# LayerScale on one core: the stores released by VectorE's third-piece product and not by a load's landing

## Chip, cores and metric

One core of a Trainium2 chip runs the kernel. The metric is the device time of one execution in microseconds (us); lower is better. Before the change the median of three runs is 119.76 us (119.63 to 119.88). No host time is in it.

## The reference

```python
B, S, D = 1024, 16, 512          # all bfloat16
def reference(x, y, gamma):      # x, y: (B, S, D), gamma: (D)
    return x + gamma * y
```

x, y and the output are 16.78 MB each. The kernel must read 33.56 MB and write 16.78 MB of HBM, and it does one product and one sum per element.

## The kernel before

The tensors are seen as 16384 rows of 512 elements, 128 for each partition. "Rows 4 to 68" below are rows of this count in a partition. `BLOCKS` cuts the 128 into blocks of 4, 64 and 60 rows; inside a block each partition's rows are contiguous in HBM, so a transfer of rows 4 to 68 is 128 runs of 64 KB. `PIECES` cuts the same 128 rows for VectorE: pieces 0 to 4 are rows 0 to 8, 8 to 24, 24 to 68, 68 to 120 and 120 to 128.

Nothing is scheduled: every engine's order is written out by hand.

- `SP` lists the transfers that SyncE issues, in order: y 0 to 4, y 4 to 68, x 4 to 68, y 68 to 128, x 68 to 120, x 120 to 128. `ACT` lists those of ScalarE's queue: x 0 to 4, gamma, and then the three stores, rows 4 to 68, 0 to 4 and 68 to 128. ScalarE computes nothing. The profile calls SP's DMA queue q1 and ScalarE's q10.
- `y_sb` holds all 128 rows of y, is multiplied and added to in place, and is what the stores read. `x_sb` has no room for all of x: the last number of an x load is its place there. x 68 to 120 goes where rows 24 to 68 (piece 2) lay, and x 120 to 128 where piece 0's lay; `frees` makes these loads wait for the sums of those pieces (`s_add`).
- `DVE` lists VectorE's instructions: products ("m") of pieces 0, 1, 2, sums ("a") of 2, 0, 1, products of 3 and 4, sums of 3 and 4. A product is line 180, a sum line 189. Each waits for its load by a semaphore (`need`), and a sum waits for the products before it (`s_dve`).
- TensorE broadcasts gamma to all partitions by a matmul with ones (L152), and VectorE copies the result to `gamma_sb` (L154).
- `ring` issues one engine's transfers. A store waits for `s_go` once, ahead of the first store, and for as many sums in `s_add` as its rows need. For the first store these are three sums, for the last all five.

`RELEASE` names what sets `s_go`. Before, it is the load of x's rows 68 to 120. TensorE waits for that load and passes it on, to ScalarE (`s_go`) and to VectorE (`s_rel`), whose sum of piece 3 needs the same load:

```python
    _take(s_load[RELEASE], 16, nc.tensor)
    nc.tensor.sem_inc(s_go, 1)
    nc.tensor.sem_inc(s_rel, 1)
```

`_take` waits for a semaphore and takes the count off again. At the end SyncE waits for ScalarE's end, all sums and all three stores.

Of the kernel before, what the change touches and what calls it, by code (L numbers as in the profile page):

```python
# [22 lines left out]

HOLD, AHEAD = ('y', 0, 4), (2, 1)

RELEASE = ('x', 68, 120, 24)

DVE = [('m', 0), ('m', 1), ('m', 2), ('a', 2), ('a', 0), ('a', 1), ('m', 3), ('m', 4), ('a', 3), ('a', 4)]
MULT, ADD = mybir.AluOpType.mult, mybir.AluOpType.add


def _take(sem, n, eng):


    return eng.wait_ge(sem, n).then_inc(sem, -n)  # L35


def kernel(
    tc: tile.TileContext,
    x: bass.AP,  # L40
    y: bass.AP,
    gamma: bass.AP,
    out: bass.AP,
):

    nc = tc.nc
    P = nc.NUM_PARTITIONS
    tc.close()  # L50
    tc.compile()  # L51

    xf = x.flatten_outer_dims()
    yf = y.flatten_outer_dims()
    of = out.flatten_outer_dims()
    N, D = xf.shape
    rows = N // P
    n = len(PIECES)
    assert sum(PIECES) == rows
    starts = [sum(PIECES[:c]) for c in range(n + 1)]  # L60
    dt = xf.dtype
    edges = [sum(BLOCKS[:c]) for c in range(len(BLOCKS) + 1)]
    assert edges[-1] == rows

    def rows_of(t, a, b):

        c = max(c for c in range(len(BLOCKS)) if edges[c] <= a)
        assert b <= edges[c + 1]
        block = t[P * edges[c] : P * edges[c + 1]].rearrange("(p n) d -> p n d", p=P)
        return block[:, a - edges[c] : b - edges[c], :]  # L70

    gamma_row = nc.alloc_sbuf_tensor("gamma_row", [1, D], dt).ap()
    ones_row = nc.alloc_sbuf_tensor("ones_row", [1, P], dt).ap()
    gamma_sb = nc.alloc_sbuf_tensor("gamma_sb", [P, D], dt).ap()
    y_sb = nc.alloc_sbuf_tensor("y_sb", [P, rows, D], dt).ap()
    x_loads = [w for w in ACT + SP if w[0] == "x"]
    y_loads = [w for w in SP + ACT if w[0] == "y"]
    stores = [w for w in SP + ACT if w[0] == "s"]
    for loads in (x_loads, y_loads, stores):
        assert sum(w[2] - w[1] for w in loads) == rows  # L80
    x_rows = max(w[3] + w[2] - w[1] for w in x_loads)
    x_sb = nc.alloc_sbuf_tensor("x_sb", [P, x_rows, D], dt).ap()
    gamma_ps = nc.alloc_psum_tensor("gamma_ps", [P, D], mybir.dt.float32).ap()

    sem = nc.alloc_semaphore
    s_gamma, s_ones, s_ps, s_dve = sem("s_gamma"), sem("s_ones"), sem("s_ps"), sem("s_dve")
    s_load = {w: sem("s_" + "_".join(map(str, w[:2]))) for w in x_loads + y_loads}
    s_held = {nc.sync: sem("s_held_sp"), nc.scalar: sem("s_held_act"), nc.vector: sem("s_held_dve")}
    s_add, s_go, s_rel, s_end, s_out = sem("s_add"), sem("s_go"), sem("s_rel"), sem("s_end"), sem("s_out")
    added = [a for kind, *a in DVE if kind == "a"]  # L90
    order = {a[0]: k for k, a in enumerate(added)}

    def meets(a, b, c, d):
        return a < d and c < b

    def pieces_of(a, b):
        return [c for c in range(n) if meets(starts[c], starts[c + 1], a, b)]

    def x_at(row):
        return next(w[3] + row - w[1] for w in x_loads if w[1] <= row < w[2])  # L100

    def frees(w):

        c = set()
        for v in x_loads[: x_loads.index(w)]:
            lo, hi = max(v[3], w[3]), min(v[3] + v[2] - v[1], w[3] + w[2] - w[1])
            if lo < hi:
                c |= set(pieces_of(v[1] + lo - v[3], v[1] + hi - v[3]))
        return sorted(c)

    early = []

    def ring(eng, what, n_early, n_ahead):

        known, went = 0, False
        for k, w in enumerate(what):
            kind = w[0]
            if k == n_ahead:
                _take(s_held[eng], 1, eng)
            need = frees(w) if kind == "x" else pieces_of(w[1], w[2]) + list(w[3:]) if kind == "s" else []  # L120
            need = max((order[c] + 1 for c in need), default=0)
            if kind == "s" and not went:
                _take(s_go, 1, eng)
                went = True
            if need > known:
                eng.wait_ge(s_add, need)
                known = need
            if kind == "g":
                i = eng.dma_start(out=gamma_row, in_=gamma.unsqueeze(0)).then_inc(s_gamma, 16)
            elif kind == "x":  # L130
                to = x_sb[:, w[3] : w[3] + w[2] - w[1], :]
                i = eng.dma_start(out=to, in_=rows_of(xf, w[1], w[2])).then_inc(s_load[w], 16)
            elif kind == "y":
                r = slice(w[1], w[2])
                i = eng.dma_start(out=y_sb[:, r, :], in_=rows_of(yf, w[1], w[2])).then_inc(s_load[w], 16)
            else:
                r = slice(w[1], w[2])
                i = eng.dma_start(out=rows_of(of, w[1], w[2]), in_=y_sb[:, r, :]).then_inc(s_out, 16)
            if k < n_early:
                early.append(i.ins)  # L140

    ring(nc.sync, SP, EARLY[0], AHEAD[0])
    ring(nc.scalar, ACT, EARLY[1], AHEAD[1])


    nc.vector.memset(ones_row, 1.0).then_inc(s_ones, 1)  # L146
    _take(s_load[HOLD], 16, nc.tensor)
    for s_one in s_held.values():
        nc.tensor.sem_inc(s_one, 1)
    _take(s_ones, 1, nc.tensor)  # L150
    _take(s_gamma, 16, nc.tensor)
    nc.tensor.matmul(gamma_ps, ones_row, gamma_row, start=True, stop=True).then_inc(s_ps, 1)  # L152
    _take(s_ps, 1, nc.vector)
    nc.vector.tensor_copy(out=gamma_sb, in_=gamma_ps).then_inc(s_dve, 1)  # L154
    _take(s_dve, 1, nc.vector)

    _take(s_load[RELEASE], 16, nc.tensor)
    nc.tensor.sem_inc(s_go, 1)
    nc.tensor.sem_inc(s_rel, 1)

    landed, open_mults = set(), 0

    def need(loads, c):
        for w in loads:
            if w not in landed and meets(starts[c], starts[c + 1], w[1], w[2]):
                if w == RELEASE:
                    _take(s_rel, 1, nc.vector)
                elif w == HOLD:
                    _take(s_held[nc.vector], 1, nc.vector)
                else:  # L170
                    _take(s_load[w], 16, nc.vector)
                landed.add(w)

    for kind, *args in DVE:
        c = args[0]
        yt = y_sb[:, starts[c] : starts[c + 1], :]
        if kind == "m":
            need(y_loads, c)
            g = gamma_sb[:, None, :].to_broadcast([P, PIECES[c], D])
            nc.vector.tensor_tensor(out=yt, in0=yt, in1=g, op=MULT).then_inc(s_dve, 1)  # L180
            open_mults += 1
        else:
            need(x_loads, c)
            if open_mults:
                _take(s_dve, open_mults, nc.vector)
                open_mults = 0
            at = x_at(starts[c])
            xt = x_sb[:, at : at + PIECES[c], :]
            nc.vector.tensor_tensor(out=yt, in0=xt, in1=yt, op=ADD).then_inc(s_add, 1)  # L189


    nc.scalar.sem_inc(s_end, 1)
    _take(s_end, 1, nc.sync)
    _take(s_add, n, nc.sync)
    _take(s_out, 16 * len(stores), nc.sync)

    main = nc.main_func.blocks[0].instructions
    names = {i.name for i in early}
    for b in nc.main_func.blocks[1:]:
        for i in [i for i in b.instructions if i.name in names]:  # L200
            b.instructions.remove(i)
    for k, i in enumerate(early):
        main.insert(1 + k, i)
# [30 lines left out]
```

## Time and profile before

| what | value |
|---|---|
| median of the runs | 119.76 us |
| the profiled execution: its span, first to last instruction | 118.2 us |
| around the span, by the median | 1.5 us |
| VectorE busy | 70.1 us (59% of the span) |
| DMA queues q1 + q10, share of 16 engines | 64.8% + 33.9% |
| HBM read and written | 33.56 MB, 16.78 MB |
| x 68 to 120: issued, to landing | 55.37, 21.7 us |
| x 120 to 128: issued, to landing | 57.58, 22.0 us |
| stores issued | 77.41, 77.81, 94.43 us |
| sum of piece 3 / of piece 4 start | 78.17 / 92.11 us |

Times of a row are counted from the span's start. The profile shows one execution, whose own time is its span and what lies around it; the median is over other executions. The matmul, the copy and the small memsets together take under 2 us. The DMA share is the busy time of the 16 DMA engines; a transfer of 128 partitions runs on all of them, 8 partitions each. In a window's row the columns are its edges, its length, the busy time and instructions of PE, PEld, DVE and POOL, the granted TensorE clock, the DMA share and GB/s. A DMA packet is counted in the window where it starts, so short windows swing above and below 1.00.

### The profile page before, as it was taken

The numbers are of one execution on the slowest core, as the hardware profiler recorded it, in microseconds if no ns is written. First come the engines' busy times: TensorE is split into PE (matmuls) and PEld (weight loads), VectorE is DVE, ScalarE is ACT, GpSimd is POOL, SyncE is SP. The second block draws the span as 40 slices with busy tenths as digits, with TensorE's granted clock in tenths as the row PEclk, the third lists the DMA queues.
The fourth block names the chain that finished last, engine by engine and source line by source line (L and its number), as shares of the span: only waits on it lengthen the run. The fifth ranks groups of instructions, "written<-read, shape, count | busy, mean of one in ns | idle before, by whom it ended". The sixth has DMA issues, their size and how long they took to land. (4 is left out here: it accounts for less than half of the span.)

```text
span 118.2 us, 91 instructions
## 1 busy us (share of the span) xinstructions
PE 0.6 (0%) x1; PEld 0.1 (0%) x1; DVE 70.1 (59%) x12; POOL 0.2 (0%) x4
## 2 busy tenths in 40 slices
PE   0000100000000000000000000000000000000000
PEld 0000000000000000000000000000000000000000
DVE  0000200089999969999999999999999900000000
POOL 0000000000000000000000000000000000000000
DMA  6999889988899879879969696898899889799793
GB/s 248 461 666 399 355 355 399 665 355 355 355 599 466 355 333 624 374 333 499 499 288 576 288 576 288 360 637 355 355 576 488 355 355 510 333 582 416 333 499 166
DMA packets 1442, 50.33 MB, mean 426 GB/s; under 512 B 161, under 2 KB 162, under 8 KB 546
## 3 DMA queue, kind: packets, MB, share of 16 engines
q1 hardware_dynamic: 864, 33.03, 64.8%
q10 hardware_dynamic: 578, 17.30, 33.9%
HBM read 33.56 MB, written 16.78 MB: 426 GB/s over the span
## 5 line engine op out<-in xcount | busy, mean ns | idle before, releaser
L180 DVE TENSOR_TENSOR y_sb<-y_sb,gamma_sb 128x4096 bf16<-128x4096 bf16 (+3 forms) x5 | 34.7, 6981 | 10.9 <-DVEq L35 10.9
L189 DVE TENSOR_TENSOR y_sb<-x_sb,y_sb 128x4096 bf16<-128x4096 bf16 (+3 forms) x5 | 34.7, 6981 | 1.2 <-DVEq L35 1.1
L154 DVE CAST gamma_sb<-gamma_ps 128x512 bf16<-128x512 f32 x1 | 0.7, 692 | 10.2 <-DVEq L35 10.2
L146 DVE MEMSET ones_row<- 1x128 bf16 x1 | 0.2, 165 | 2.0 <-PEq L51 2.0
L152 PE MATMUL gamma_ps<-gamma_row,ones_row 1*128 1x512 bf16 x1 | 0.6, 581 | 11.6 <-PEq L35 11.6
L152 PEld LDWEIGHTS gamma_ps<-gamma_row,ones_row 1*128 1x128 bf16 x1 | 0.1, 101 | 11.6 <-issue 11.6
L218 POOL MEMSET const-bfloat16-1.0<- 128x1 bf16 x1 | 0.1, 101 | 0.0
L218 POOL MEMSET const-uint8-127<- 128x1 uint8 x1 | 0.1, 101 | 0.0
L218 POOL MEMSET const-float32-0.0<- 128x1 f32 x1 | 0.1, 98 | 0.2 <-issue 0.2
L218 POOL MEMSET const-float32-1.0<- 128x1 f32 x1 | 0.1, 98 | 0.0
## 6 DMA issues: line engine op xcount, KB each, us to landing
y_sb<-in_y_dram SPq DMA_DIRECT2D x1, 7680.0 KB, 57.3
out_dram<-y_sb ACTq DMA_DIRECT2D x1, 7680.0 KB, 23.8
x_sb<-in_x_dram SPq DMA_DIRECT2D x1, 6656.0 KB, 21.7
x_sb<-in_x_dram SPq DMA_DIRECT2D x1, 1024.0 KB, 22.0
y_sb<-in_y_dram SPq DMA_DIRECT2D x1, 512.0 KB, 3.4
x_sb<-in_x_dram ACTq DMA_DIRECT2D x1, 512.0 KB, 4.2
out_dram<-y_sb ACTq DMA_DIRECT2D x1, 512.0 KB, 22.3
y_sb<-in_y_dram SPq DMA_DIRECT2D x1, 23.4
```

Source lines behind the costliest of these rows:

```text
L146: nc.vector.memset(ones_row, 1.0).then_inc(s_ones, 1)
L152: nc.tensor.matmul(gamma_ps, ones_row, gamma_row, start=True, stop=True).then_inc(s_ps, 1)
L154: nc.vector.tensor_copy(out=gamma_sb, in_=gamma_ps).then_inc(s_dve, 1)
L180: nc.vector.tensor_tensor(out=yt, in0=yt, in1=g, op=MULT).then_inc(s_dve, 1)
L189: nc.vector.tensor_tensor(out=yt, in0=xt, in1=yt, op=ADD).then_inc(s_add, 1)
L218: nc = _bacc.Bacc("TRN2", target_bir_lowering=False, num_devices=1)
```

## The change

`RELEASE` becomes the number of a piece, 3. Its product (y's rows 68 to 120) increments `s_go` when it ends, in place of `s_dve`. ScalarE's first store waits for that. TensorE's wait and its two increments go, `s_rel` with them; the sum of piece 3 now waits for the load of x's rows 68 to 120 itself, and for `s_go`, because its operand is that product's result. Since two engines wait for `s_go`, neither takes the count off; SyncE does at the end. No transfer, piece or order is changed.

```diff
-RELEASE = ('x', 68, 120, 24)
+RELEASE = 3
...
             if kind == "s" and not went:
-                _take(s_go, 1, eng)
+                eng.wait_ge(s_go, 1)
                 went = True
...
-    _take(s_load[RELEASE], 16, nc.tensor)
-    nc.tensor.sem_inc(s_go, 1)
-    nc.tensor.sem_inc(s_rel, 1)
-
-    landed, open_mults = set(), 0
+    landed, open_mults, going = set(), 0, False
...
             if w not in landed and meets(starts[c], starts[c + 1], w[1], w[2]):
-                if w == RELEASE:
-                    _take(s_rel, 1, nc.vector)
-                elif w == HOLD:
+                if w == HOLD:
...
-            nc.vector.tensor_tensor(out=yt, in0=yt, in1=g, op=MULT).then_inc(s_dve, 1)
-            open_mults += 1
+            nc.vector.tensor_tensor(out=yt, in0=yt, in1=g, op=MULT).then_inc(s_go if c == RELEASE else s_dve, 1)
+            if c == RELEASE:
+                going = True
+            else:
+                open_mults += 1
...
                 open_mults = 0
+            if going:
+                nc.vector.wait_ge(s_go, 1)
+                going = False
...
     _take(s_add, n, nc.sync)
+    _take(s_go, 1, nc.sync)
     _take(s_out, 16 * len(stores), nc.sync)
```

More of the change, by code (lines that the diff above doesn't have):

```diff
@@ L88 @@
     s_held = {nc.sync: sem("s_held_sp"), nc.scalar: sem("s_held_act"), nc.vector: sem("s_held_dve")}
-    s_add, s_go, s_rel, s_end, s_out = sem("s_add"), sem("s_go"), sem("s_rel"), sem("s_end"), sem("s_out")
+    s_add, s_go, s_end, s_out = sem("s_add"), sem("s_go"), sem("s_end"), sem("s_out")
     added = [a for kind, *a in DVE if kind == "a"]
```

## The prediction

> **What bounds the kernel now.** I read the page's first two parts for which resource is full, then the same resource stage by stage, then the issues and their landings, then the order of instructions around the stores.
>
> The first parts of the page:
>
> ```profile
> span 118.2 us, 91 instructions
> ...
> PE 0.6 (0%) x1; PEld 0.1 (0%) x1; DVE 70.1 (59%) x12; POOL 0.2 (0%) x4
> ...
> q1 hardware_dynamic: 864, 33.03, 64.8%
> q10 hardware_dynamic: 578, 17.30, 33.9%
> ```
>
> VectorE works for 59% of the span. The two DMA queues (q1 is SP's, q10 is ScalarE's) fill 64.8 + 33.9 = 98.7% of the time of the 16 DMA engines. The windows, with edges put where the kind of traffic changes, show whether the missing 1.3% lies in the middle (the last two columns are the DMA share and GB/s):
>
> ```profile
> 3.60:60.50 56.90, 0.58 (x1) 0.10 (x1) 36.17 (x7) 0.00 (x0) 1.00 1.00 434
> 60.50:76.30 15.80, 0.00 (x0) 0.00 (x0) 15.80 (x3) 0.00 (x0) 1.00 1.00 432
> 76.30:78.73 2.43, 0.00 (x0) 0.00 (x0) 2.28 (x2) 0.00 (x0) 1.00 1.04 438
> 78.73:99.30 20.57, 0.00 (x0) 0.00 (x0) 15.66 (x2) 0.00 (x0) 1.00 1.00 433
> 99.30:117.90 18.60, 0.00 (x0) 0.00 (x0) 0.00 (x0) 0.00 (x0) 1.00 0.97 422
> ```
>
> It does not. From 3.6 us on the engines are full to the end, and loads (second line) and stores (fourth) run at one rate, 432 and 433 GB/s. The third line is the place of the change: the last loads give way to the first stores there, with no hole. So the time is the bytes over the rate, and only a hole or a dearer byte can move it.
>
> ```profile
> y_sb<-in_y_dram SPq DMA_DIRECT2D x1, 7680.0 KB, 57.3
> out_dram<-y_sb ACTq DMA_DIRECT2D x1, 7680.0 KB, 23.8
> x_sb<-in_x_dram SPq DMA_DIRECT2D x1, 6656.0 KB, 21.7
> x_sb<-in_x_dram SPq DMA_DIRECT2D x1, 1024.0 KB, 22.0
> ...
> out_dram<-y_sb ACTq DMA_DIRECT2D x1, 512.0 KB, 22.3
> ```
>
> The 6656 KB load is x's rows 68 to 120 ("x68"), the 1024 KB load x's rows 120 to 128 ("x120"). x68 is issued at 55.37 and lands at 55.37 + 21.7 = 77.1; x120 at 57.58, lands at 79.6. The timeline between 75 and 80 us:
>
> ```profile
> 61.80 16.22 DVE L180 TENSOR_TENSOR y_sb<-y_sb,gamma_sb 128x26624 bf16<-128x26624 bf16 x2
> 77.41 0.86 ACTq L138 DMA_DIRECT2D out_dram<-y_sb  x2
> 78.17 14.02 DVE L189 TENSOR_TENSOR y_sb<-x_sb,y_sb 128x26624 bf16<-128x26624 bf16 x1
> ```
>
> The first row is the product of piece 3 (14.02 us by its group's row) and that of piece 4 (2.29). Piece 3's product signals its end at 75.83 in the trace's semaphore records, x68's landing passes TensorE and releases ScalarE at 77.30, and the first store is issued at 77.41.
>
> **The change, part by part.** The profiled execution's span is 118.2 us; the runs shown have a median of 119.76, so some 1.5 us lie around the span, and nothing here touches them.
>
> *TensorE's wait and two increments go.* They are the hops from 77.06 (landing) to 77.30 and 77.45; the engine does nothing after them. Worth nothing by itself.
>
> *The first store's release.* ScalarE now waits for piece 3's end: 75.83 and not 77.30, 1.47 us earlier. From release to issue took 0.11 us, so I expect the issue at 75.9. Its other wait, for three sums, was met at 61.89. The rows 0 to 4 follow at once as before, and the last store still waits for all sums. In the sum this is worth nothing: the windows show no hole for earlier stores to fill. What they do is to push x120 aside, so that is the cost to work out.
>
> *How far x120 is pushed.* The packet records of the trace give each engine's work. Before, every engine ran its eight 8 KB packets of x120 unbroken (309 ns each, first starts 76.27 to 76.71), then its 4-byte semaphore packet, and 6 ns later its first 64 KB store packet (2.42 us; first starts 78.73 to 79.16). No store came between them. If the stores come 1.48 us earlier (77.41 − 75.93), they can get in at most 1.48 / 0.306 = 4.8 packets before the old end: four x120 packets and the semaphore packet are left on each engine. x68 itself is through (76.71) before that: first stores at 77.25 to 77.68. The release of the sum of piece 3 is not harmed.
>
> Now the order of service. Two places in the trace have both queues loaded. At 2.2 to 2.8 us y's rows 0 to 4 (q1) and x's rows 0 to 4 (q10) alternate: from the first q10 packet on, q1 starts 24 more and q10 about as many. And gamma's single 1 KB packet on q10 goes at 8.63, then one 64 KB packet of q1 (2.45), then gamma's semaphore packet at 11.12: one for one. By that row x120 lands at 77.68 + 5 × 2.42 (five store packets ahead of the semaphore) + 4 × 0.31 + 0.4 (from the last packet to the landing, as before) = 91.4 us, 12 us later than now.
>
> *Who waits for that.* Only the sum of piece 4, and it starts at 92.11 because the 14.02 us sum of piece 3 ends there. 91.4 is just under it. The slack behind is larger: the last store's first packets start at 99.29 to 99.73, when the queue has emptied. From a landing to that takes 0.14 (landing to start, as for the first product) + 2.28 + 0.02 + 1.0 (issue to first packet, as for the very first load) = 3.44, so x120 may land as late as 95.8 before an engine goes idle. An estimate from these rows: 4.4 us of cover. Cost: nothing.
>
> *VectorE's queue.* The sum of piece 3 waits for x68 itself and for one more semaphore. Each queued wait takes some 0.11 us there (43.23, 43.35, 43.45 in the trace). Piece 4's product ends at 78.03 and hides the first; the extra one may move the sum from 78.17 to 78.28, and the last issue from 94.43 to 94.54. Covered by about 4 us (94.54 + 1.0 against 99.29). SP's added wait at the end passes at about 94.9, ahead of a wait that ends at 118.2; nothing is queued behind it but that.
>
> *What a switch between loads and stores costs.* Before switches once, load to store, for nothing (6 ns). After does it some five times on each engine, and store to load stands nowhere in the trace. From above: the first packets of the kernel, into cold engines, took up to 352 ns where 159 is normal, 0.19 more: 5 × 0.19 = 0.97 us. A nearer row: gamma, squeezed between two 64 KB packets, took 46 ns, and the next packet 2467 for 2418, together some 0.1. From below: a load that runs inside a store's time would save up to 4 × 0.306 = 1.2 us; on each engine the records follow end to start, and nothing overlaps. I take zero, the row of the one switch seen, and keep both ends.
>
> Sum: 0 + 0 + 0; span 118.2, time 119.8.
>
> *A rule that speaks against it.* The records show single packets alternating. The Trainium skill, page "DMA: Bandwidth & Descriptors", section "Queues, rings and completion order", says that an engine drains a whole packet, some 9 to 17 descriptors, of one queue before it turns to the next. By that the eight rows of the first store would run in one turn and the time would be that of the starved case below; the alternation at 2.2 us is the measurement against it.
>
> **The rivals.**
>
> *Starved load (slower).* The stores get two or more packets for each of x120's. Then the eight store packets of the large store all go before x120 is through: 77.68 + 8 × 2.42 = 97.0, + 4 × 0.31 + 0.4 = 98.7. The sum of piece 4 ends at 98.7 + 0.14 + 2.28 = 101.1, the last store's packets start at 102.2 where the queue was empty at 99.29: 2.9 us of idle engines, 122.7. It decides from a landing of x120 past 95.8. For it: gamma was issued at 3.90 and let two 64 KB packets start before its turn, so a short packet can wait long. Against: the second time it waited for one only.
>
> *Dear switches (slower).* DMA records stay without holes but some are longer: 0.1 to 0.97 us more, 119.9 to 120.7. For it: the cold first packets. Against: the free switch at 78.7 and the 159 ns kept in the alternation.
>
> *Cheap overlap (faster).* Loads move inside stores' time: up to 1.2 us, 118.6. Against: loads and stores run at the same 432 and 433 GB/s, end to end.
>
> *It does not do what it says.* ScalarE is held by something else until 77.4. It has nothing queued before and its sums are long done; 119.8 again.
>
> **How the numbers follow.** Forecast 119.8, no change: 0.40. Starved load 0.26, dear switches 0.22 (0.18 of it past the bound), cheap overlap 0.10, not as said 0.02. Two-tenths of a per cent, 0.24 us, is about what a measurement of this kernel can tell from no change (its runs span 119.63 to 119.88). Slower: 0.26 + 0.18 = 0.44; faster 0.10; same 0.40 + 0.04 + 0.02 = 0.46. The range must reach the starved case: 119.5 to 122.7, which leaves out the overlap case and little more. The likeliest case's own range is 119.6 to 120.0.
>
> **What would show it.** Right: first store issued near 75.9, x120 landing near 91 (33 to 34 us after its issue and not 22.0), x68 still at 77.1, the sum of piece 4 still at about 92.2, last issue at 94.4 to 94.6, DMA share 1.00 in every window from 3.6 to 117.9. Starved: x120 lands past 95.8, VectorE idles before its last sum, and a window near 100 us shows a lower share. Dear switches: the window from 77 to 92 moves fewer GB/s than 433. Wrong altogether: x68 landing later than 77.1, or the first store's packets before 77.

## The result, and the profile after

The changed kernel takes 120.59 us (120.56 to 120.68) where the kernel before took 119.72 us on the same chip: a ratio of 1.0071 with a 95% interval of [1.0057, 1.0086], so 0.87 us slower. The forecast was no change at 119.8 with a range to 122.7. The range holds the time; the likeliest case (119.6 to 120.0) does not, and its mechanism was wrong.

The page after, the lines that answer to those shown before:

```profile
span 119.2 us, 89 instructions
...
PE 0.6 (0%) x1; PEld 0.1 (0%) x1; DVE 70.1 (59%) x12; POOL 0.2 (0%) x4
...
q1 hardware_dynamic: 864, 33.03, 64.9%
q10 hardware_dynamic: 578, 17.30, 33.6%
```

The page alone says where the time is, once shares are turned into times. Loads (q1): 0.649 × 119.2 = 77.4 us, where it was 0.648 × 118.2 = 76.6. Stores (q10): 40.1 and 40.1. Bytes and packets are the same, so the loads became dearer by some 0.8 us of the average engine (rounded shares; the packet records sum to 0.71), and the stores did not. The windows, with the edges of before (DMA share and GB/s at the end):

```profile
60.50:76.30 15.80, 0.00 (x0) 0.00 (x0) 15.80 (x3) 0.00 (x0) 1.00 1.00 431
76.30:78.73 2.43, 0.00 (x0) 0.00 (x0) 2.28 (x2) 0.00 (x0) 1.00 0.99 337
78.73:99.30 20.57, 0.00 (x0) 0.00 (x0) 15.77 (x2) 0.00 (x0) 1.00 0.99 426
```

The third window of before was 1.04 and 438. Now the engines are as busy as ever there, 0.99, and move 337 GB/s. That is not a hole but slow packets, and a busy share cannot show it. The issues:

```profile
out_dram<-y_sb ACTq DMA_DIRECT2D x1, 7680.0 KB, 24.7
x_sb<-in_x_dram SPq DMA_DIRECT2D x1, 6656.0 KB, 21.7
x_sb<-in_x_dram SPq DMA_DIRECT2D x1, 1024.0 KB, 22.8
```

x's rows 68 to 120 take 21.7 us as before, rows 120 to 128 ("x120") 22.8 and not 22.0, and the last store 24.7 and not 23.8. The timeline around the stores:

```profile
75.96 0.85 ACTq L138 DMA_DIRECT2D out_dram<-y_sb  x2
78.27 14.03 DVE L189 TENSOR_TENSOR y_sb<-x_sb,y_sb 128x26624 bf16<-128x26624 bf16 x1
```

The stores are issued 1.45 us earlier. VectorE's sum of piece 3 starts at 78.27, the whole of VectorE's work being 0.1 us later in this execution from its first product on.

The packet records of the trace say what happened on the engines. The eight 8 KB packets of x120 took 309 ns each before, all 128 of them. After, the 46 that start before 77.33 take 309 to 321; of the 82 that start later, 46 take 338 to 844, the last of them at 79.41. On the average engine that is 0.62 us; the other 0.1 of the 0.71 is in the kernel's first 4 KB load packets, which the change does not touch. The latest engine needed 3.34 us from its first x120 packet to its first store packet instead of 2.45, 0.89 more, and it sets the end: its records, followed from end to start, are the last in both traces (to 117.85 before, to 118.86 after). No store packet came between: as before, each engine's first 64 KB packet follows the last load (79.47 to 80.18; before 78.73 to 79.16) and takes 2.42 us as ever.

### The profile page after: what moved, and what is told of

It reads as the page before. It is cut to its first block, busy times and chain, and to the rows that moved or that the text cites. A ratio compares the mean times of both kernels' runs of the same rounds, so it can differ in the third digit from the quotient of the medians.

```text
span 119.2 us, 89 instructions
## 1 busy us (share of the span) xinstructions
PE 0.6 (0%) x1; PEld 0.1 (0%) x1; DVE 70.1 (59%) x12; POOL 0.2 (0%) x4
## 6 DMA issues: line engine op xcount, KB each, us to landing
out_dram<-y_sb ACTq DMA_DIRECT2D x1, 7680.0 KB, 24.7
x_sb<-in_x_dram SPq DMA_DIRECT2D x1, 6656.0 KB, 21.7
x_sb<-in_x_dram SPq DMA_DIRECT2D x1, 1024.0 KB, 22.8
out_dram<-y_sb ACTq DMA_DIRECT2D x1, 512.0 KB, 24.7
```

## The experiments

The questions: why do loads run slow that are in front of the stores, and why did packets not alternate? Where a run has a median, the second number is its ratio to the kernel before on the same chip, with its 95% interval. The excess of load packets in a run is read from its one profiled execution.

**Is it the issue of the second store?** The small store goes last.

```diff
-ACT = [..., ('s', 4, 68), ('s', 0, 4), ('s', 68, 128)]
+ACT = [..., ('s', 4, 68), ('s', 68, 128), ('s', 0, 4)]
```

> The changed kernel, with the 512 KB store of rows 0 to 4 moved behind the last store; the 8 MB store is still released at 75.8. In the changed kernel the 8 KB load packets of x's rows 120 to 128 took 0.34 to 0.85 us instead of 0.31 between 77.3 and 78.9 us. Theory A (a load's packet is slowed while a store waits open beside it on the same DMA engine): the same slow packets, 120.6 us. Theory B (it is the issue of the second store, 0.4 us after the first, whose descriptors are being made just then): no slow packets or far fewer, 119.7 to 119.9. Theory C (only small load packets suffer, each by a fixed price): as A, 120.6.

120.73 us, 1.0080 [1.0067, 1.0093]. The slow packets are there, from 77.22 on, and cost 0.88 us of the average engine. Theory B is out: the second store's issue is not needed for the loss.

**Is it a price of small packets?** The last loads swapped, so that 52 KB packets stand in front of the stores.

```diff
-    ('x', 68, 120, 24),
-    ('x', 120, 128, 0),
+    ('x', 120, 128, 0),
+    ('x', 68, 120, 24),
```

> The changed kernel, with the two last x loads swapped: rows 120 to 128 are loaded ahead of rows 68 to 120, so that at the release (75.8) the loads in flight are the 52 KB packets of rows 68 to 120, which end near 78.8. The sum of piece 3 then starts near 79.6 and the last store is issued near 95.9, still ahead of the emptying of the queue at 99.3. Theory A (loads are slowed while a store is open, whatever their size): the last 52 KB packets are longer than 1.97 us by 0.6 to 0.9, 120.4 to 120.6. Theory B (making of the second store's descriptors): the same, 120.4 to 120.6. Theory C (a price for each small packet): at most two packets pay, 119.7 to 119.9. Should packets of the two queues alternate after all, x's rows 68 to 120 land some 2.4 us later, near 82, and the time is 119.9 to 120.3.

120.94 us, 1.0113 [1.0075, 1.0151], with more scatter (120.54 to 122.34) than the others, which I cannot explain. On each engine one 52 KB packet, the last, takes up to 2.97 us instead of 1.97, 0.84 on the average (the profiled execution, 120.54, is the fastest of the six). A loss of the same size in one packet: no price for each small one, so theory C is out.

**When does it begin?** Releases between the two kernels. First the landing of x's rows 68 to 120, without TensorE:

```diff
-                _take(s_go, 1, eng)
+                eng.wait_ge(s_load[RELEASE], 16)
...
-                    _take(s_rel, 1, nc.vector)
+                    nc.vector.wait_ge(s_load[RELEASE], 16)
```

> The kernel before, but ScalarE and VectorE wait for the landing of x's rows 68 to 120 themselves, without TensorE between: stores released near 77.1, 0.2 us earlier than before and 1.2 us later than in the changed kernel. By the changed kernel's records, slow packets begin 1.37 us after the first issue, here at 78.5, where each engine has one or two of the eight small packets left. Theories A and C: 0.1 to 0.3 us of it, 119.8 to 120.0. Theory B: the second store's descriptors are made when nearly all loads are through, 119.7 to 119.8.

Then the end of the product of piece 4:

```diff
-RELEASE = 3
+RELEASE = 4
```

> The changed kernel with the release put at the end of the product of piece 4 (78.03) in place of piece 3 (75.83): first store issued at 78.1, 0.7 us later than before. All theories: no slow load packets, all eight at 0.31 us. First store packet not before 78.1 + 1.3 = 79.4, where the loads end at 78.7 to 79.2: a hole of 0.3 to 0.7 us on every engine, 120.0 to 120.4. If it gives 119.7, the time from issue to the first packet is shorter than the 1.3 us which the trace of before shows as its upper bound, and stores were open beside the loads before the change too.

And two in between, by a cut in that product:

```diff
-RELEASE = 3
+RELEASE, HEAD = 4, 2      # or 4: rows of piece 4's product in its first part, which sets s_go
```

> The changed kernel with the product of piece 4 cut in two, rows 120 to 122 and 122 to 128; the first part releases the stores, so they are issued near 76.5, between the changed kernel (75.96) and the kernel before (77.41). Theory R (a store whose descriptors are in place while an engine still has loads to finish ahead of it slows these loads, whatever queue, once, by a bounded amount; nothing is lost where it comes less than some 0.8 us before their end): the loss grows with the lead, so a part of 0.87, 120.0 to 120.4. Theory S (a step: the whole loss once the store comes ahead of the last fetched load): 120.5 or 119.75, nothing between.

> The same with the cut at row 124, stores issued near 77.1. Theory R: the lead is some 0.8 us at the most, 119.7 to 119.9. Theory S: 119.75, or 120.5 if the step lies between here and 77.33.

| released by | first store issued | median us | ratio [interval] | x120: issue to landing | 8 KB load packets, excess of the average engine |
|---|---|---|---|---|---|
| product of piece 3 (the change) | 75.96 | 120.59 | 1.0071 [1.0057, 1.0086] | 22.8 | 0.62 |
| 2 rows of piece 4 | 76.57 | 120.26 | 1.0045 [1.0033, 1.0056] | 22.5 | 0.39 |
| 4 rows of piece 4 | 77.24 | 119.76 | 1.0002 [0.9993, 1.0010] | 22.0 | 0.01 |
| landing, directly | 77.33 | 119.71 | 0.9996 [0.9988, 1.0005] | 22.0 | 0.00 |
| landing by way of TensorE (before) | 77.41 | 119.72 to 119.78 | 1 | 22.0 | 0.00 |
| product of piece 4 | 78.20 | 119.86 | 1.0006 [0.9997, 1.0015] | 22.3 | 0.00 |

The loss grows with how early the stores come and is gone at 77.24. It is not a step, so theory S is out. In these rows the packets of x120 end on the latest engine, where undisturbed, at 79.2 to 79.6; a store issued up to some 2 us ahead of that costs nothing. TensorE's hop is worth nothing. For the release by the landing itself, theories A and C had expected 119.8 to 120.0, with slow packets 1.37 us after the issue; none came, though loads ran to 79.35, 2 us after it. The run of piece 4 did not show the hole I expected: its first store packet follows 0.97 us after the issue, right behind the loads, so the 1.3 us which I had as an upper bound is above the real time. (The 22.3 of its x120 comes from a few longer 52 KB load packets near 61 to 63, ahead of any store's issue.)

**Is it the other queue?** All stores on SyncE, behind the loads in one queue.

```diff
+    ('s', 4, 68), ('s', 0, 4), ('s', 68, 128),     # at the end of SP
-... ('s', 4, 68), ('s', 0, 4), ('s', 68, 128)]     # in ACT
```

> The changed kernel, with the three stores issued by SyncE behind its last load, so on the same DMA queue (q1) as the loads, and still released at 75.8 by the product of piece 3. Theory A (a load beside a store that is open in another queue of the same engine): nothing can pass the loads, no slow packets, 119.6 to 119.9. Theory E (making the descriptors of the 8 MB store, or the moment itself, slows the engines): slow load packets from 77.3 as in the changed kernel, 120.5 to 120.9.

120.90 us, 1.0093 [1.0079, 1.0106]. My theory A fell here: in one queue, where nothing can pass, the loads are slowed all the same, 0.88 us of the average engine. Its issues:

```profile
out_dram<-y_sb SPq DMA_DIRECT2D x1, 7680.0 KB, 25.0
x_sb<-in_x_dram SPq DMA_DIRECT2D x1, 6656.0 KB, 21.7
x_sb<-in_x_dram SPq DMA_DIRECT2D x1, 1024.0 KB, 23.1
```

The 23.1 of x120 is the mark again. So a store that is queued behind loads is enough; no second queue is needed. The number is that of theory E. Its two causes are tried below: the descriptors of the 8 MB store by a run in which only the 512 KB store comes early, the moment itself by a run in which a load is issued then and no store.

**How far does it go, and do packets alternate at all?** The stores go with their sums, at 62.1, and nothing waits for `s_go` any more.

```diff
-                eng.wait_ge(s_go, 1)
```

> The changed kernel without the release: the stores of rows 4 to 68 and 0 to 4 go as soon as their sums are done (61.9), 14 us earlier, with all of x's rows 68 to 128 still to be loaded. Theory A1 (a load is slowed once, by a bounded amount, when a store opens beside it, 0.65 to 0.9 us an engine): one slow load packet on each engine near 63 to 65, then full speed; 120.4 to 120.9. Theory A2 (loads run slow for as long as a store is open beside them): slow packets until the loads end, several us lost, over 123. Alternation of whole packets, as my prediction had it: x's rows 68 to 120 land near 96 and not 77, the last store is issued near 114 into an empty queue, 130 or more.

130.50 us, 1.0895 [1.0880, 1.0910]. The windows of this run:

```profile
60.50:63.00 2.50, 0.00 (x0) 0.00 (x0) 2.50 (x2) 0.00 (x0) 1.00 1.44 618
63.00:68.00 5.00, 0.00 (x0) 0.00 (x0) 5.00 (x1) 0.00 (x0) 1.00 0.84 255
68.00:94.00 26.00, 0.00 (x0) 0.00 (x0) 10.87 (x3) 0.00 (x0) 1.00 1.01 436
94.00:110.00 16.00, 0.00 (x0) 0.00 (x0) 15.56 (x2) 0.00 (x0) 1.00 0.39 164
```

Three things are in it. One load packet on each engine, starting at 64.7 to 65.1, takes 3.1 to 3.4 us and not 1.97, and it is the one just in front of the first store packet: a loss of 1.3 us, once. Then the engines alternate for 26 us, one 52 KB load packet, one 64 KB store packet, at 1.97 and 2.42 us each: 436 GB/s, so a switch costs nothing in either direction, and loads that share an engine with waiting stores run at full speed here. And the loads land late (37.5 us for rows 68 to 120), the sums follow, and the last window is mostly empty (0.39): that is where the 10 us are. So A1's one slow packet and the alternation of the prediction both came. But the first store packet came only 5.7 us after its issue (62.10 to 67.82); each engine first ended the load packet that it had begun and ran two more.

**Does the store's packet size matter?** First the small store ahead of the large one, then the small one alone.

```diff
-ACT = [..., ('s', 4, 68), ('s', 0, 4), ('s', 68, 128)]
+ACT = [..., ('s', 0, 4), ('s', 4, 68), ('s', 68, 128)]
```

> The changed kernel with the two first stores swapped: the 512 KB store (4 KB packets, eight on each engine) is issued at 75.9, the 8 MB store (64 KB packets) 0.4 us later. If the lost 0.65 to 0.9 us is data of a store read ahead of its turn, small packets fit whole and can be written between the loads: store packets are seen between those of x's rows 120 to 128, which then land near 81, and the time is 119.8 to 120.6 by how much of the 8 MB store is read ahead besides. If the loss belongs to any store that opens beside a load: no store packet before the loads' end, 120.5 to 120.9.

120.58 us, 1.0066 [1.0052, 1.0079]; slow loads from 77.6 on, 0.61 us, and no store packet ahead of the loads' end.

```diff
+            if w == ('s', 4, 68):
+                eng.wait_ge(s_load[LAST], 16)      # on top of the run before; LAST = x 68 to 120
```

> Only the 512 KB store (rows 0 to 4, 4 KB packets) is released by the product of piece 3 at 75.8; the 8 MB store waits for the landing of x's rows 68 to 120, 77.1. If it is the direction (any store ahead of its turn): slow load packets from 77.3 on, 120.3 to 120.6. If it is the 64 KB packets: 119.7 to 119.9.

120.53 us, 1.0065 [1.0052, 1.0078]; 0.66 us of slow loads, with only 4 KB store packets released early. The size of the store's packets makes no difference in these runs, nor is the issue of the 8 MB store needed.

**Is it stores, or any transfer that stands behind?** A load in their place, and the stores behind it.

```diff
+ACT = [('x', 0, 4, 0), ('g',), ('d', 8, 24), ('s', 4, 68), ...]    # d: x rows 8 to 24 once more, at s_go
...
-                eng.wait_ge(s_go, 1)
+                eng.wait_ge(s_load[LAST], 16)      # the first store
```

> At the end of the product of piece 3 (75.8) ScalarE's queue issues not the stores but a load that is not needed: x's rows 8 to 24 once more (2 MB, 16 KB packets, into space that is free). The stores wait for the landing of x's rows 68 to 120, as before the change, and stand behind that load. 2.10 MB more at 433 GB/s are 4.84 us. If the loss comes from a store beside a load (opposite directions): no loss here, 119.75 + 4.84 = 124.6, from 124.4 to 124.8. If any second queue opened beside the loads costs it: slow packets from 77.3 on, 125.3 to 125.5.

125.94 us, 1.0512 [1.0498, 1.0526]: neither number. x120 ran at full speed (309 ns a packet, one of 358, landing after 22.0 us) beside the open load, which the first theory said. But 1.3 us are lost all the same, further on:

```profile
76.30:79.20 2.90, 0.00 (x0) 0.00 (x0) 2.72 (x2) 0.00 (x0) 1.00 1.04 441
79.20:85.20 6.00, 0.00 (x0) 0.00 (x0) 6.00 (x1) 0.00 (x0) 1.00 1.14 399
85.20:123.00 37.80, 0.00 (x0) 0.00 (x0) 9.45 (x2) 0.00 (x0) 1.00 0.99 430
```

The second window is the unneeded load, now itself the loads in front of stores that were issued at 77.33. Its 16 KB packets take 0.61 us until 81.3, and then up to 1.36; 1.25 us of the average engine. So the slowing is not tied to the issue (here it begins 4 us after it) nor to the release: it goes with the last loads in front of a waiting store. The test of that is to let the stores come just ahead of that load's end:

```diff
-                eng.wait_ge(s_load[LAST], 16)
+                eng.wait_ge(s_part, 1)             # set by the first 17 of 52 rows of the sum of piece 3
```

> The run with the unneeded 2 MB load at 75.9, but the stores wait for the first 17 rows of the sum of piece 3 (near 83.0) and not for the load's landing at 77.1, so they are issued some 1 us before the unneeded load ends and not 7 us. Theory R: its packets stay at 0.61 us, and the 1.3 us lost in the run before (125.94 against 119.78 + 4.84) come back, less a hole of up to 0.4: 124.6 to 125.0. If the unneeded load itself costs them: 125.9 again.

124.94 us (1.0445 [1.0419, 1.0470]), 1.0 less than 125.94, and 0.4 above 119.72 + 4.84, as much as I had allowed for a hole; whether it is one, no trace shows. The stores came 6 us later and the kernel got faster. The profiled execution of this run took 125.89, where the other five took 124.73 to 124.98; it has slow load packets from 79.0 to 82.4 (up to 2.01 us for 0.61), ahead of the first store's issue at 83.38. So loads ran slow in this one execution with no store waiting, and why is open; its trace does not stand for the other five, and I read only the median.

No version beat the kernel before: its engines have no hole to fill, and the one without TensorE is the same (ratio 0.9996).

## Why the prediction was right or wrong

- *DMA sets the end, and earlier stores have no hole to fill.* Right: nothing came of the 1.45 us, in any run.
- *Release at 75.9; x's rows 68 to 120 at 77.1; sum of piece 3 near 78.3; sum of piece 4 near 92.2; last issue 94.4 to 94.6.* Right: 75.96, 77.2, 78.27, 92.2, 94.53. The extra wait of VectorE cost nothing at all: from the end of piece 4's product to the sum are 0.15 us in both traces.
- *How far x120 is pushed.* Wrong. I had it land at 91.4, by one-for-one alternation from the moment the stores are ready. It landed at 80.5. The alternation is real (the early release shows it for 26 us), but an engine that is busy with loads takes its first packet of the other queue late: 5.7 us after the issue there. The trace of before had that row, and I used only half of it: gamma's packet ran at 8.63 us, issued at 3.90, 4.7 us. (Of the two 64 KB packets that the prediction counts before gamma's turn, the first had begun at 3.72, ahead of the issue; and the packet right after gamma took 2452 ns, the 2467 being another engine's. Neither moves the sum.) Here the loads had some 3.3 us to go after the issue, less than either wait, and the stores got no turn before their end. I priced the rhythm and not the time to the first turn. What the Trainium skill says in "DMA: Bandwidth & Descriptors", "Queues, rings and completion order", of 9 to 17 descriptors to a turn does not fit either, if a record is a descriptor: with the large packets of the early release it was one and one.
- *What a switch costs.* I took zero, with 0.1 to 0.97 above. A switch does cost zero, 436 GB/s over 26 us of switching. The term that failed is the one that I had not: the loads in front of a waiting store. I had them run at 0.31 us a packet whenever the stores came. It measured 0.62 us on the average engine and 0.89 on the latest. That the result fell into the span of "dear switches" (119.9 to 120.7), which had 0.22, is an accident of size. That the range holds the time is luck too: it reached to 122.7 for starved loads, which did not come. Fewer GB/s at a full share was the right sign to look for, but not in the window that I named: 77 to 92 shows 460 GB/s (469 before), both above 433, because a packet counts where it starts. It shows from 76.30 to 78.73.
- *Starved load.* Did not happen: VectorE waited for nothing in its last sum, and x120 landed 15 us ahead of the 95.8 from which it would have told.
- *Cheap overlap.* Did not come: no record has a load inside a store's time, and no run was clearly faster.

What stays open is what the engine does in the lost time. My guess is that a store's data is fetched ahead of its turn, at the loads' expense. The loss is at most 1.3 us in these runs, comes once, shrinks with the lead, needs no second queue, and comes with small and large store packets, which would fit. But no record shows the fetch, and nothing of the loss comes back: behind the slow loads the first store packets take 2.42 us (64 KB) and 0.159 (4 KB) as in the kernel before.

## What to carry to other kernels

Where the DMA engines are full, as here, releasing a store earlier gave nothing, and where it then stood behind the last loads for more than about 2 us it cost: time the release so that the store's first packet is due as the loads run out. Read GB/s beside the busy share, and turn queue shares into times: a full engine that moves less looks the same as a good one. To price a transfer that joins a busy engine, take two numbers from the trace, how long until its first packet and how packets alternate from then on.

## What the runs showed of the hardware

- The last load packets in front of a waiting store's first packet ran slower, in the same queue (0.88 us lost) as in another (0.61 to 0.88). Once the store had its turn, loads alternated with it at full speed. A load that waited in another queue slowed none (309 ns for the 8 KB packets).
- The loss came once and grew with the lead: 0.39 us with the store issued at 76.57, 0.62 at 75.96, 1.3 with the stores 14 us early or a 2 MB load in between, none at 77.24.
- Slow load packets also came with no store waiting, in one of the six executions of the last run (up to 2.01 us for 0.61); why is open.
- Two loaded queues alternate one packet for one, 52 KB loads and 64 KB stores, at full speed for both (436 GB/s); the first packet of the queue that joins came 4.7 and 5.7 us after its issue on busy engines, and within 0.97 us where the loads had just run out.
